# Part of a short convolution as float32 matmuls by diagonal matrices, and a state product for two column blocks at a time, in a kernel of attention and two feed-forward layers

## The chip, the core and the metric

The kernel runs on one core of one Trainium2 chip. The core has a matrix engine (TensorE, PE in the profile, with its weight loads as PEld), three engines for elementwise work (VectorE as DVE, ScalarE as ACT, GpSimd as POOL) and queues that start transfers (here all on SyncE, SP). Each engine works through its own instructions in a fixed order and waits on semaphores for the others. The metric is the time of one execution on the device in microseconds (us); lower is better.

## What is computed

Three stages follow each other. B = 8 batches, H = 8 heads, S = 512 tokens, Ns = 32 state tokens, D = 64; the feed-forward layers have a model width of 512 and an inner width of 1024. The weights and the taps of the convolution come as float64, the rest as float32.

```python
# 1: attention both ways between tokens x and a state
a     = softmax(scale * x @ state.T);   xread = a @ state
a2    = softmax(scale * state @ x.T);   sread = a2 @ x
y     = concat(xread, sread)            # 576 tokens, heads side by side: 512 wide
# 2: feed-forward with a convolution over three tokens as its gate
h     = relu(y @ w_in)                  # 1024 wide
conv  = cw[0] * h[t-1] + cw[1] * h[t] + cw[2] * h[t+1]      # per column, zeros at the ends
z     = (h * sigmoid(conv)) @ w_out
# 3: feed-forward with a mix of each token and the one before it
out   = sigmoid(xr @ w_r) * (relu(xk @ w_k) ** 2 @ w_v)
```

## The kernel before

**Precision.** Nearly every large product runs in float32r, a reduced form of float32, with each operand split into a high and a low part. `mm3` issues three matmuls for one product: high by high (L112), high by low (L113), low by high (L114). The float64 weights are split on the chip by `Weights.split`: two ACT instructions (L158 absolute value, L164 sign) and six DVE instructions (L160, L161, L165, L166, L169, L170) on 128x1024 for each piece of two blocks. There are four pieces of w_in and four of w_out; two staging buffers are shared by them, so a piece is loaded when the piece two before it has been split.

**Layout.** In stage 2 the columns of h are cut into KF = 8 blocks of 128 (f), and a block stands with its 128 columns on the partitions and 512 tokens along the row. Tiles t = 0 to 7 are the 512 token rows of a batch each; tile 8 holds the state rows of all batches. A slot (t, f) goes through five steps: `g1_main` (the product hps on PE), `g1_a` (Relu to hb on ACT, then the convolution), `g1_b` (sigmoid on ACT, times h on POOL for tile 0 and on DVE otherwise, tile g), `g1_c` (g split into gs, high on ACT, low on POOL for tiles 0 to 2) and `g1_sec` (twelve matmuls into four accumulators acc). The convolution is one ACT instruction for the first tap (L441) and two SCALAR_TENSOR_TENSOR on DVE for the others (L443), each over 128x512.

**The state product.** xread @ w_in isn't formed from xread. The state is first multiplied into w_in (`Attention.m`, tile p_m in PSUM, then me or m_odd in SBUF, as high and low), and hps is the attention matrix aring by that product. For batch 0, `m(q, f0, 1)` makes one block of 128 columns at a time: twelve matmuls over 128 columns, an ACT eviction (L274) and a DVE subtraction (L275). From batch 2 on, pairs of batches share the work (`pair_m`, L234), and the results are moved to me and m_odd by DMA (L237).

**PSUM.** hps has two buffers (tag h), p_m and the small products of the attention share two (tag at), and four hold the accumulators.

**What sets the order.** The program emits slots in order and gives each group of instructions a priority (`tc.cur_priority`): 1000 per slot plus a number for the step, with the attention and the weights hung in at half slots (`at_half`). A scheduler then puts the instructions of each engine in one fixed order, by these priorities and its own times. On the start, the SP queue carries the first state, x, the first piece of w_in, the taps (`vec.load`, two transfers), mu and the first piece of w_out.

Of the kernel before, what the change touches and what calls it, by code (L numbers as in the profile page):

```python
# [8 lines left out]
F32 = mybir.dt.float32  # L9
# [3 lines left out]
AF = mybir.ActivationFunctionType  # L13
ALU = mybir.AluOpType
AX = mybir.AxisListType

LOW_ON_POOL = (0, 1, 2)
GATE_ON_POOL = (0,)


BASE = 100000
# [9 lines left out]
def tile_kernel(  # L31
# [26 lines left out]
    nc = tc.nc  # L58
    B, P, NST, H, D = x_n.shape
    KC, S = x_t.shape[1], x_t.shape[3]  # L60
    NS = st_bd.shape[2] // (2 * KC)
    KF = w_in.shape[0]
# [23 lines left out]
    op = ctx.enter_context(tc.tile_pool(name="op", bufs=1))  # L86
    dp = ctx.enter_context(tc.tile_pool(name="dp", bufs=1, space=bass.MemoryType.DRAM))
    ps_acc = ctx.enter_context(tc.tile_pool(name="ps_acc", bufs=1, space=bass.MemoryType.PSUM))
    ps_h = ctx.enter_context(tc.tile_pool(name="ps_h", bufs=2, space=bass.MemoryType.PSUM))
# [6 lines left out]
    ident = const.tile([P, P], F32, name="ident")  # L96
    vcol = const.tile([P, 3 * KF], F32, name="vcol")
# [95 lines left out]
    def load_s(b, ap):  # L193
        sT[b] = ap.tile([P, KC, 2, NS], F32, tag="sT", name="sT", bufs=3)
        nc.sync.dma_start(out=sT[b].rearrange("p c u n -> p (c u n)"), in_=st_bd[b])

    def load_t(b, ap):
        xT[b] = ap.tile([P, KC, S], F32, tag="xT", name="xT", bufs=1)
        for c in range(KC):
            nc.sync.dma_start(out=xT[b][:, c], in_=x_t[b, c])  # L200
# [203 lines left out]
    def width(t):  # L404
        return S if t < B else B * Z - 2
# [18 lines left out]
    def g1_a(t, f):  # L424
        n = width(t)
        s = st1[t, f]
        hb = s["hb"] = cp.tile([P, N + 2], F32, tag="hb", name="hb", bufs=3)
        if t < B:
            nc.gpsimd.memset(hb[:, 0:S + 2:S + 1], 0.0)  # L429
            nc.scalar.activation(hb[:, 1:1 + S], s["p"], AF.Relu)  # L430
            nc.gpsimd.tensor_copy(carry[:, f, t], hb[:, S - 1:S + 1])
        else:
            v = hb[:, :B * Z].rearrange("p (b n) -> p b n", b=B)
            nc.gpsimd.tensor_copy(v[:, :, 0:2], carry[:, f])
            nc.gpsimd.memset(v[:, :, NS + 2:], 0.0)
            nc.scalar.activation(
                v[:, :, 2:NS + 2], s["p"][:, :B * NS].rearrange("p (b n) -> p b n", b=B), AF.Relu
            )
        a = s["a"] = cp.tile([P, N], F32, tag="acc", name="cacc")
        w = [vcol[:, k * KF + f:k * KF + f + 1] for k in range(3)]  # L440
        nc.scalar.activation(a[:, :n], hb[:, 0:n], AF.Copy, scale=w[0])  # L441
        for k in (1, 2):
            nc.vector.scalar_tensor_tensor(  # L443
                a[:, :n], hb[:, k:k + n], w[k], a[:, :n], op0=ALU.mult, op1=ALU.add
            )

    def g1_b(t, f):
# [3 lines left out]
        nc.scalar.activation(g[:, :n], s["a"][:, :n], AF.Sigmoid)  # L451
        eng = nc.gpsimd if t in GATE_ON_POOL else nc.vector
        eng.tensor_tensor(g[:, :n], g[:, :n], s["hb"][:, 1:1 + n], op=ALU.mult)
# [146 lines left out]
    def at_half(k, *fns, prio=None):  # L600
        p = 500 * k - AHEAD if prio is None else prio
        half.setdefault(k, []).extend((fn, p) for fn in fns)
# [9 lines left out]
    vec = Weights([conv], 1, 3 * KF, const, "c")  # L612
    vs = const.tile([P, 2, 3 * KF], F32R, name="vs")
    load_s(0, ap)
    load_t(0, ap)
    win[0][0]()
    vec.load()
    nc.sync.dma_start(out=muc, in_=mu)
    wout[0][0]()
    make_identity(nc, ident)  # L620
# [1 line left out]
    a = Attention(0, ap)  # L622
    a.scores([ps_acc.tile([P, 512], F32, tag=f"acc{g}", name="p_s") for g in range(G)])
    a.begin()
    win[0][1]()
    a.state()
    a.m(0, 0, 1)
    for g in range(G):
        a.max1(g, nc.vector)
    for g in range(G):  # L630
# [7 lines left out]
        a.norm1(g, nc.vector)  # L638
    for g in range(G):
        a.turn1(g)  # L640
    vec.split(vs.rearrange("p l (o n) -> p l o n", o=1))
    nc.vector.tensor_tensor(vcol, vs[:, 0].bitcast(F32), vs[:, 1].bitcast(F32), op=ALU.add)
    nc.vector.tensor_scalar(om, muc, scalar1=-1.0, scalar2=1.0, op0=ALU.mult, op1=ALU.add)
    wout[0][1]()

# [35 lines left out]
    def weight_at(w, need, at):  # L681
        at_half(at, w[0], w[1], prio=500 * need - WEIGHT_AHEAD)
# [4 lines left out]
    for f in range(1, KF):  # L687
        if f % 2 == 0:
            weight_at(win[f // 2], 2 * f - 1, max(0, 2 * f - 5))
        at_half(2 * f - 1, lambda f=f: a.m(f // 2, f % 2, 1))  # L690
    for f in range(2, KF, 2):
        weight_at(wout[f // 2], 2 * f + 5, 2 * f + 2)
    at_half(0, lambda: load_s(1, ap), lambda: load_t(1, ap), prio=-500)
# [2 lines left out]
    for b in range(1, B):  # L696
# [3 lines left out]
        (2, t, f) for t in range(NT2) for f in range(KF)  # L700
    ]
    FN = {1: (g1_main, g1_a, g1_b, g1_c, g1_sec), 2: (g2_main, g2_a, g2_b, g2_c, g2_sec)}
    p2 = None
    for i in range(len(slots) + 2):
        if i < len(slots):
            ph, t, f = slots[i]
            if (ph, t, f) == (1, B - 1, 2):
                ap_cm.__exit__(None, None, None)
                p2 = ctx.enter_context(tc.tile_pool(name="p2", bufs=1))
                for k in range(0, KF, 2):  # L710
                    w = weight(w_k, "k", "wk", p2, k, 2, 2)
                    h = h2 + 2 * k
                    weight_at(w, h, h - 4)
                for k in range(0, KF, 2):
                    w = weight(w_v, "v", "wa", wp, k, 2, 4)
                    h = h2 + 2 * k + 4
                    weight_at(w, h + 1, h - 3)
                for k in range(0, KC, 2):
                    w = weight(w_r, "r", "wb", wp, k, 2, 2)
                    h = h2 + 8  # L720
# [84 lines left out]
```

## Time and profile before

| | us |
|---|---|
| median of 3 runs (898.67 to 899.33) | 899.1 |
| the profiled execution | 901.15 |
| its span from first to last instruction | 899.2 |
| PE busy in the span | 850.8 (95%) |
| DVE busy | 564.0 (63%) |
| ACT busy | 531.2 (59%) |
| POOL busy | 118.8 (13%) |
| mean granted clock of PE | 0.974 of full |

The shares are averages over stages that differ: PE's 95% says little on the first 75 us, and DVE's 63% holds a stretch in which it is full. So such a profile is read by stretch first, then by the waits of the engine that ends last, then by the instructions around one place. "Idle before" is the time an engine stood still ahead of an instruction, with what ended it. Durations of one engine overlap by some hundredths of a microsecond, since its instructions are pipelined; what one costs in a full stretch is nearer to the distance between starts. PE clock 1.00 is 2.4 GHz and 0.50 is 1.2 GHz.

### The profile page before, as it was taken

The page shows a single profiled execution, that of the slowest core. Times are in us where ns is not written, and L with a number is a line of the kernel's source. Part 1 is how long each engine was busy: PE and PEld are TensorE (multiplying, and loading weights), DVE is VectorE, ACT ScalarE, POOL GpSimd, SP SyncE. Part 2 cuts the span into 40 slices and gives each one's busy share as a digit, 9 for nine tenths or more (in the row PEclk, how much of TensorE's full clock was granted, in tenths as well). Part 3 has the DMA queues.
Part 4 walks back from the last instruction along what each step waited for, and adds up shares of the span by engine and source line. Part 5 has one row for each costly group of instructions (what it writes and reads, how often), then busy time and mean ns, then how long its engine had stood idle before and what let it go on. Part 6 is the DMA issues. An engine that isn't in the chain of part 4 may idle for free.

```text
span 899.2 us, 12003 instructions
## 1 busy us (share of the span) xinstructions
PE 850.8 (95%) x4440; PEld 692.3 (77%) x4440; DVE 564.0 (63%) x950; ACT 531.2 (59%) x929; POOL 118.8 (13%) x223
## 2 busy tenths in 40 slices
PE   3749999999999997999999999999999999999997
PEld 1628777768777875789988888888888888888886
DVE  6899897699879987999784543523424244332221
ACT  4557686578577757777666755635556364553431
POOL 2313753342011112121000000000000000000000
PEclk7778999999999999999999999999999999999999
DMA  9682224544451537536731101111001111011010
GB/s 341 228 348 96 77 95 118 162 131 118 139 166 59 168 127 246 175 122 252 273 128 47 28 20 47 47 47 48 18 29 48 47 47 47 1 36 48 0 47 36
DMA packets 50842, 95.76 MB, mean 106 GB/s; under 512 B 9056, under 2 KB 31072, under 8 KB 48736
## 3 DMA queue, kind: packets, MB, share of 16 engines
q1 hardware_dynamic: 50784, 95.00, 32.0%
q8 instruction: 35, 0.57, 0.3%
q14 instruction: 23, 0.19, 0.1%
HBM read 64.54 MB, written 17.86 MB: 92 GB/s over the span
## 4 chain that ended last, share of the span: by engine, by line
PE 83%; DVE 8%; ACT 3%; issue 2%; DMA 2%; POOL 1%; SPq 0%; DVEq 0%; ACTq 0%; POOLq 0%
PE acc L113 13%; PE acc L114 13%; PE acc L112 13%; PE kps L112 7%; PE kps L113 7%; PE kps L114 7%; PE rps L114 3%; PE rps L113 3%; PE rps L112 3%; PE hps L112 3%; PE hps L114 3%; PE hps L113 3%; DVE cacc L443 2%; PE p_s L284 2%; PE p_m L113 1%
## 5 line engine op out<-in xcount | busy, mean ns | idle before, releaser
L568 DVE TENSOR_TENSOR ks<-k,ks 128x512 fp32r<-128x512 f32 (+1 forms) x72 | 47.7, 662 | 118.2 <-ACT ks L567 117.8
L443 DVE SCALAR_TENSOR_TENSOR cacc<-hb,vcol,cacc 128x512 f32<-128x512 f32 (+1 forms) x144 | 111.8, 788 | 15.5 <-ACT cacc L441 14.9
L113 PE MATMUL acc<-gs,out 128*128 128x512 f32 (+1 forms) x288 | 110.6, 386 | 0.0
L112 PE MATMUL kps<-xk,k 128*128 128x512 f32 (+1 forms) x288 | 110.0, 384 | 0.2 <-ACT k L554 0.2
L113 PE MATMUL kps<-xk,k 128*128 128x512 f32 (+1 forms) x288 | 110.2, 382 | 0.0
L114 PE MATMUL kps<-xk,k 128*128 128x512 f32 (+1 forms) x288 | 109.8, 382 | 0.0
L114 PE MATMUL acc<-gs,out 128*128 128x512 f32 (+1 forms) x288 | 109.6, 384 | 0.0
L112 PE MATMUL acc<-v,ks 128*128 128x512 f32 x272 | 106.0, 392 | 0.0
L113 PE MATMUL acc<-v,ks 128*128 128x512 f32 x272 | 105.9, 389 | 0.0
L114 PE MATMUL acc<-v,ks 128*128 128x512 f32 x272 | 105.7, 392 | 0.0
L112 PE MATMUL acc<-gs,out 128*128 128x512 f32 (+1 forms) x288 | 94.3, 389 | 4.3 <-ACT gs L459 4.3
L533 DVE SCALAR_TENSOR_TENSOR mix<-yt,muc,mix 128x384 f32<-128x384 f32 (+7 forms) x128 | 61.1, 500 | 47.7 <-ACT mix L531 47.2
L567 ACT ACTIVATE ks<-k 128x512 fp32r<-128x512 f32 (+1 forms) x72 | 43.6, 605 | 69.8 <-PE acc L114 69.6
L531 ACT ACTIVATE mix<-yt,om 128x384 f32<-128x384 f32 (+7 forms) x128 | 61.5, 517 | 32.2 <-DMA yt<-y 15.8
L554 ACT ACTIVATE k<-kps 128x512 f32<-128x512 f32 (+1 forms) x72 | 40.9, 569 | 48.9 <-PE kps L114 48.7
L112 PEld LDWEIGHTS acc<-gs,out 128*128 128x128 f32 x288 | 53.7, 192 | 16.1 <-ACT gs L459 6.1
L113 PEld LDWEIGHTS acc<-gs,out 128*128 128x128 f32 x288 | 54.8, 190 | 12.8 <-POOL hb L429 0.8
L114 PEld LDWEIGHTS acc<-gs,out 128*128 128x128 f32 x288 | 54.9, 191 | 10.8 <-issue 0.8
L112 PEld LDWEIGHTS kps<-xk,k 128*128 128x128 f32 x288 | 54.1, 188 | 10.8 <-ACT k L554 0.7
L113 PEld LDWEIGHTS kps<-xk,k 128*128 128x128 f32 x288 | 54.4, 189 | 10.1
L114 PEld LDWEIGHTS kps<-xk,k 128*128 128x128 f32 x288 | 54.3, 188 | 10.1
L451 ACT ACTIVATE g<-cacc 128x512 f32<-128x512 f32 (+1 forms) x72 | 43.8, 609 | 27.5 <-DVE cacc L443 19.4
(133 smaller groups left out, 1771.3 us busy)
## 6 DMA issues: line engine op xcount, KB each, us to landing
out<-r SPq DMA_DIRECT2D x34, 256.0 KB, 2.1
xT<-x_t SPq DMA_DIRECT2D x32, 256.0 KB, 4.0
xn<-x_n SPq DMA_DIRECT2D x8, 1024.0 KB, 5.4
y<-yo SPq DMA_DIRECT2D x8, 1024.0 KB, 4.8
me<-m SPq DMA_DIRECT2D x48, 128.0 KB, 2.4
m_odd<-m SPq DMA_DIRECT2D x48, 128.0 KB, 2.4
raw<-w_in SPq DMA_DIRECT2D x8, 512.0 KB, 6.0
raw<-w_out SPq DMA_DIRECT2D x8, 512.0 KB, 5.7
```

The source lines that it names most:

```text
L112: nc.tensor.matmul(ps, lh, rh, start=start and k == 0, stop=False)
L113: nc.tensor.matmul(ps, lh, rl, start=False, stop=False)
L114: nc.tensor.matmul(ps, ll, rh, start=False, stop=stop and k == last)
L284: nc.tensor.matmul(self.v["s", g][NS * j:NS * (j + 1), :], sT[self.b][r, h // 2, h % 2], xT[self.b][r, h // 2], start=True, stop=True,)
L443: nc.vector.scalar_tensor_tensor(a[:, :n], hb[:, k:k + n], w[k], a[:, :n], op0=ALU.mult, op1=ALU.add)
L451: nc.scalar.activation(g[:, :n], s["a"][:, :n], AF.Sigmoid)
L531: nc.scalar.activation(tmp[:, o:o + m], y[:, c, q - 1:q - 1 + m], AF.Copy, scale=om[:, i:i + 1])
L533: nc.vector.scalar_tensor_tensor(tmp[:, o:o + m], y[:, c, q:q + m], muc[:, i:i + 1], tmp[:, o:o + m], op0=ALU.mult, op1=ALU.add,)
L554: nc.scalar.activation(k[:, :n], s["p"][:, :n], AF.Relu)
L567: nc.scalar.activation(ks[:, 0, :n], s["k2"][:, :n], AF.Copy)
L568: nc.vector.tensor_tensor(ks[:, 1, :n], s["k2"][:, :n], ks[:, 0, :n].bitcast(F32), op=ALU.subtract)
```

## The change

For the first five blocks of tile 0 the convolution goes to PE. Each tap of a block becomes a 128x128 diagonal matrix (tile diag, fifteen of them, made by ACT from the identity matrix), and three float32 matmuls, not float32r, add the three shifted copies of hb into a PSUM tile cps of tag h; the sigmoid reads cps. Blocks 5 to 7 of tile 0 and all other tiles keep L441 and L443. For that the taps are loaded ahead of x and split ahead of all other DVE work. And `m` of batch 0 makes two blocks per call: half as many matmuls, each over 256 columns, and half as many evictions, each over 128x512.

```diff
+CONV_ON_PE = 5
...
+        if t == 0 and f < CONV_ON_PE:
+            a = s["a"] = ps_h.tile([P, 512], F32, tag="h", name="cps")
+            for k in range(3):
+                nc.tensor.matmul(a, diag[:, 3 * f + k], hb[:, k:k + S], start=k == 0, stop=k == 2)
+            return
         a = s["a"] = cp.tile([P, N], F32, tag="acc", name="cacc")
...
     load_s(0, ap)
+    vec.load()
     load_t(0, ap)
     win[0][0]()
-    vec.load()
...
+    vec.split(vs.rearrange("p l (o n) -> p l o n", o=1))
+    nc.vector.tensor_tensor(vcol, vs[:, 0].bitcast(F32), vs[:, 1].bitcast(F32), op=ALU.add)
+    diag = op.tile([P, 16, P], F32, tag="o8", name="diag")
+
+    def diagonals(f):
+        for k in range(3):
+            nc.scalar.activation(diag[:, 3 * f + k], ident, AF.Copy, scale=vcol[:, k * KF + f:k * KF + f + 1])
+
     win[0][1]()
     a.state()
-    a.m(0, 0, 1)
+    a.m(0, 0, 2)
...
-    vec.split(vs.rearrange("p l (o n) -> p l o n", o=1))
-    nc.vector.tensor_tensor(vcol, vs[:, 0].bitcast(F32), vs[:, 1].bitcast(F32), op=ALU.add)
+    diagonals(0)
...
         if f % 2 == 0:
             weight_at(win[f // 2], 2 * f - 1, max(0, 2 * f - 5))
-        at_half(2 * f - 1, lambda f=f: a.m(f // 2, f % 2, 1))
+            at_half(2 * f - 1, lambda f=f: a.m(f // 2, 0, 2))
+        if f < CONV_ON_PE:
+            at_half(2 * f - 1, lambda f=f: diagonals(f))
```

The lines of the changed kernel stand 2 lines lower up to the convolution and 7 to 16 lower behind it, so that L443 before has no counterpart for these blocks, L160 is L162, L164 is L166 and L451 is L458.

DVE around the first two blocks' convolution and the second piece of w_in, before (in_153 and out_222 are the split weights, cacc the convolution):

```order
L170 SCALAR_TENSOR_TENSOR out_222<-mid,raw 128x1024
L443 SCALAR_TENSOR_TENSOR cacc<-hb,vcol,cacc 128x512 x2
L160 TENSOR_SCALAR raw<-raw 128x1024
L169 TENSOR_SCALAR mid<-mid 128x1024
L161 TENSOR_SCALAR raw<-raw 128x1024
L165 TENSOR_TENSOR in_153<-raw 128x1024
L443 SCALAR_TENSOR_TENSOR cacc<-hb,vcol,cacc 128x512
L166 TENSOR_SCALAR raw<-in_153 128x1024
L443 SCALAR_TENSOR_TENSOR cacc<-hb,vcol,cacc 128x512
L371 TENSOR_SCALAR sr<-p_sr,s_151 128x128
L170 SCALAR_TENSOR_TENSOR in_153<-mid,raw 128x1024
```

The same place now:

```order
L172 SCALAR_TENSOR_TENSOR out_226<-mid,raw 128x1024
L162 TENSOR_SCALAR raw<-raw 128x1024
L171 TENSOR_SCALAR mid<-mid 128x1024
L163 TENSOR_SCALAR raw<-raw 128x1024
L167 TENSOR_TENSOR in_163<-raw 128x1024
L168 TENSOR_SCALAR raw<-in_163 128x1024
L172 SCALAR_TENSOR_TENSOR in_163<-mid,raw 128x1024
```

The four convolution instructions are gone, and sr (L371) has moved behind this piece.

ACT at the same place, before (g is the gate, L158 and L164 are the weight split's two steps):

```order
L430 ACTIVATE hb<-hps 128x512
L441 ACTIVATE cacc<-hb,vcol 128x512
L158 ACTIVATE raw<-raw 128x1024
L356 ACTIVATE a2T<-p_a_311 128x512
L430 ACTIVATE hb<-hps 128x512
L164 ACTIVATE raw<-raw 128x1024
L451 ACT_TABLE_LOAD
L451 ACTIVATE g<-cacc 128x512
```

And now:

```order
L358 ACTIVATE a2T<-p_a_303 128x512
L432 ACTIVATE hb<-hps 128x512
L160 ACTIVATE raw<-raw 128x1024
L458 ACT_TABLE_LOAD
L458 ACTIVATE g<-cps 128x512
L166 ACTIVATE raw<-raw 128x1024
L432 ACTIVATE hb<-hps 128x512
```

The sigmoid of the first block (L451, now L458) and its table load have moved ahead of the weight split's second step, and the second block's Relu behind both.

PE where the third block's second product begins, before (acc are the accumulators, with out_496 the split piece of w_out):

```order
L112 MATMUL hps<-aring,me_108 128x512
L113 MATMUL hps<-aring,me_108 128x512
L112 MATMUL acc_435<-gs,out_496 128x512
L112 MATMUL acc_436<-gs,out_496 128x512
L112 MATMUL acc_437<-gs,out_496 128x512
L112 MATMUL acc_438<-gs,out_496 128x512
L112 MATMUL p_m<-in_339,aux 128x128
```

And now:

```order
L116 MATMUL p_m<-in_334,aux 128x256
L444 MATMUL cps<-hb,diag 128x512 x3
L114 MATMUL acc_430<-gs,out_479 128x512
L114 MATMUL acc_431<-gs,out_479 128x512
L114 MATMUL acc_432<-gs,out_479 128x512
L114 MATMUL acc_433<-gs,out_479 128x512
L114 MATMUL p_m<-in_163,aux 128x256
```

The fourth block's convolution (cps) now stands directly ahead of the third block's second product, and that block's hps, of which two matmuls stood here, is all ahead of it.

## Rows read from the trace of the kernel before

**Rows 1.** Busy us (instructions): PE, PEld, DVE, ACT, POOL; PE clock, DMA share, GB/s.

```profile
30.00:50.00 20.00, 13.57 (x120) 9.78 (x123) 16.84 (x19) 12.42 (x16) 6.98 (x9) 0.91 0.64 241
50.00:75.00 25.00, 14.00 (x61) 10.76 (x54) 24.76 (x42) 15.29 (x21) 6.92 (x6) 0.59 0.74 283
75.00:130.00 55.00, 54.59 (x351) 44.46 (x350) 50.58 (x74) 39.44 (x69) 31.99 (x42) 1.00 0.25 86
130.00:200.00 70.00, 64.88 (x432) 49.08 (x431) 53.31 (x90) 45.24 (x76) 26.72 (x43) 1.00 0.47 132
```

**Rows 2.** Waits of PE up to 200 us: total us, times, longest.

```profile
PE p_srT L380 <- ACT e L315: 8.4, 1, 8.4
...
PE hps L112 <- DMA me<-m: 3.1, 2, 1.5
```

**Rows 3.** Timeline (start, us, engine, line, operation): exponentials, third block.

```profile
60.60 0.68 ACT L315 ACTIVATE e<-p_s,s 128x512 f32<-128x512 f32 x1
...
67.39 0.63 ACT L459 ACTIVATE gs<-g 128x512 fp32r<-128x512 f32 x1 [1.70 <-POOL g L453]
...
68.08 2.07 PE L112 MATMUL acc<-gs,out 128*128 128x512 f32 x4 [1.11 <-ACT gs L459]
```

**Rows 4.** Busy time by stretch, columns as in rows 1: the half clock.

```profile
60.00:74.50 14.50, 11.14 (x42) 9.46 (x43) 14.39 (x27) 9.65 (x15) 5.23 (x4) 0.50 0.62 227
```

**Rows 5.** Timeline of PE at 134 us.

```profile
134.24 0.44 PE L354 MATMUL p_a<-ident,e 128*128 128x128 f32 x2 [0.43 <-DVE m L234]
```

**Rows 6.** By shape, 28-90 us (xcount, busy us, mean ns); then timelines.

```profile
L443 DVE SCALAR_TENSOR_TENSOR cacc<-hb,vcol,cacc 128x512 f32<-128x512 f32 x11 | 12.3, 1116 | 2.6 <-ACT cacc L441 2.5
...
56.66 0.75 DVE L443 SCALAR_TENSOR_TENSOR cacc<-hb,vcol,cacc 128x512 f32<-128x512 f32 x1
...
86.28 1.78 DVE L443 SCALAR_TENSOR_TENSOR cacc<-hb,vcol,cacc 128x512 f32<-128x512 f32 x1
...
85.78 1.74 POOL L461 TENSOR_TENSOR gs<-g,gs 128x512 fp32r<-128x512 f32 x1 [1.27 <-ACT gs L459]
```

**Rows 7.** Timeline of ACT, DVE and SP around the second piece of w_in.

```profile
30.06 0.60 ACT L430 ACTIVATE hb<-hps 128x512 f32<-128x512 f32 x1 [1.17 <-PE hps L114]
...
33.29 1.18 ACT L164 ACTIVATE raw<-raw 128x1024 f32<-128x1024 f32 x1
...
35.41 1.22 DVE L165 TENSOR_TENSOR in<-raw 128x1024 fp32r<-128x1024 f32 x1 [0.53 <-DVE raw L161]
...
41.92 0.33 SPq L138 DMA_DIRECT2D raw<-w_out  x1
...
48.96 1.14 ACT L158 ACTIVATE raw<-raw 128x1024 f32<-128x1024 f32 x1 [4.29 <-DMA raw<-w_out]
```

**Rows 8.** By shape, 28-90 us: low part of the state product, DVE.

```profile
L275 DVE TENSOR_TENSOR me<-p_m,me 128x256 fp32r<-128x256 f32 x6 | 2.5, 416 | 0.0
```

**Rows 9.** Timeline of ACT and SP at the start.

```profile
4.34 0.51 ACT L255 ACTIVATE aux<-sT 128x128 fp32r<-128x128 f32 x2
11.60 0.63 ACT L321 ACTIVATE q<-q 128x512 f32<-128x512 f32 x1 [6.76 <-DVE q L309]
...
5.23 0.54 SPq L138 DMA_DIRECT2D raw<-conv  x1
```

**Rows 10.** Timeline of PE: products of 128 and 256 columns, and scores.

```profile
78.33 0.28 PE L114 MATMUL p_m<-in,aux 128*128 128x128 f32 x1
78.44 0.28 PE L112 MATMUL p_m<-in,aux 128*128 128x128 f32 x1
...
83.07 0.28 PE L113 MATMUL p_m<-in,aux 128*128 128x256 f32 x1
83.19 0.29 PE L114 MATMUL p_m<-in,aux 128*128 128x256 f32 x1
...
107.23 1.94 PE L284 MATMUL p_s<-xT,sT 64*32 64x512 f32 x16
109.11 0.50 PE L112 MATMUL hps<-aring,m_odd 128*128 128x512 f32 x1
```

## The prediction, made before the change was run

> **What bounds the kernel now.** I read the busy time by stretch first [rows 1]. The reader should see two regimes. From 75 us on TensorE (PE) has no idle time to speak of, at full clock: 54.6 of 55 us busy up to 130 us, 64.9 of 70 us up to 200. Before that VectorE (DVE) is full and PE is not: between 50 and 75 us DVE works 24.8 of 25 us and PE 14.0, at a mean granted clock of 0.59. So the kernel is a feed phase, in which DVE splits float64 weights, runs the attention of two batches and the convolution, and then a long matmul stream. Whatever ends the feed phase earlier by x us moves the whole stream by x, and whatever adds work to PE after it is added to the end.
>
> The waits of PE name the feeder [rows 2]: the longest after the start, 8.4 us, is a transpose that waits until the exponentials have released a PSUM buffer, and these stand behind DVE's maxima. Then I followed the third block (number 2) of tile 0. Its gate lands as gs at 67.39 us, 1.70 us of ACT's idle time before it being POOL's product, and PE starts its second product at 68.08 us [rows 3]. From there PE never runs dry, but it runs at half clock: 0.50 over 60 to 74.5 us [rows 4]. 68.08 us is the place against which I set the change. A second place is 134 us, where PE has caught up with DVE again: a transpose waits 0.43 us for the state product's low part (L234) that DVE had in its queue [rows 5]. What DVE does not gain by then, PE cannot keep.
>
> **The change on DVE.** Ten SCALAR_TENSOR_TENSOR of L443 go. Eleven of them between 28 and 90 us took 12.3 us, 1.116 us each; an undisturbed one took 0.75 us, and one beside a POOL subtraction that ran from 85.78 to 87.5 us took 1.78 us [rows 6]. That extra time belongs to the collision with POOL, whose instructions all stay. The Trainium skill (GPSIMD Engine Reference, Specifications) says the same, that POOL shares its SBUF interfaces with VectorE and collides with instructions that have two SBUF inputs; by that rule the next DVE instruction pays, and the six below are worth 4.5 us and no more, which would make the time 893.3.
>
> - Blocks 2 to 4, six instructions: 6 x 0.75 = 4.5 us at least, 6 x 1.116 = 6.7 us at most. DVE has no idle time there [rows 1], so they count in full. I take 5.0, near the undisturbed price.
> - Blocks 0 and 1, four instructions: 3.0 us by the undisturbed price, but here DVE is busy 16.8 of 20 us, so part of it only turns into waiting. The wait that can take its place is visible in the order of ACT: the Sign step L164 of the second w_in piece, which started at 33.29 us and let DVE's product L165 start at 35.41 [rows 7], now stands behind the first sigmoid, which waits for the first convolution on PE. Relu ends at 30.7 us in either kernel; three float32 matmuls (2.8 us at full clock, 5.6 at half, below) end at 33.6 or 36.4, a sigmoid of 0.6 follows, and L164 starts at 34.3 to 37.1 instead of 33.29. L165 is then 0.1 to 2.9 us later than now (L164 takes 1.18), while the two convolution steps that stood between it and the end of that split (some 2.85 us with their collisions) are gone. The split ends 2.8 us earlier to 0.1 later. This is worth following, because the next w_out load is issued when it ends, at 41.92 us, and ACT waits 4.29 us for it, until 48.96 [rows 7]: a gain there is passed on by the load. I take 2.0, bounds -0.5 to 3.0.
> - The state product: eight evictions of 128x256 at 0.416 us [rows 8], 3.3 us, become four of 128x512. At the 0.75 us of the other 128x512 instruction that is 3.0, so 0.3 is saved; 0 to 1.7, between nothing and half.
> - The start: the two loads of the taps go ahead of the four of x. The first took 0.54 us of SP's time where it stood [rows 9], so two take some 1.1, and scores, maxima and the first weights all come behind them. I take -1.0, bounds -1.1 to 0. The taps' small DVE steps move with them into the time before the first transpose, in which DVE has nothing to do, so they cost nothing.
>
> Sum on DVE: 5.0 + 2.0 + 0.3 - 1.0 = **6.3 us**; ends 2.9 (4.5 - 0.5 + 0 - 1.1) and 11.4 (6.7 + 3.0 + 1.7).
>
> **On ACT.** Five L441 go, fifteen diagonals come. Two copies of 128x128 took 0.51 us, so fifteen take 15 x 0.255 = 3.8 us. The order puts all fifteen ahead of the first exponential, where ACT idles 6.76 us [rows 9]: taps landed by some 4.5 us (an estimate: the state, issued just ahead of them, let ACT copy it at 4.34), seven short DVE steps, diagonals from about 6.7 to 10.5, the exponential due at 11.6 plus the later start. Hidden, with 2 us to spare; without that cover up to 3.8 us on the first chain.
>
> **On PE.** The trace has no full float32 matmul. The nearest row is the score product: eight matmuls over 512 columns (two records each) held PE from 107.23 to 109.11 us [rows 10], 1.88 us. Run one after another that is 0.235 each, 0.7 a block; run four beside each other it is two rounds of 0.94. I take 0.94: each uses 64 rows and 32 columns of the array, and four of them don't overlap. The Trainium skill (FP8 and Floating Point Precision, TensorE Precision Notes) says that true FP32 makes four passes; float32r starts every 0.12 us at 256 columns, so by that rule one costs 4 x 0.24 = 0.96, and the low end is out. So a block costs 2.8 us at full clock and 5.6 at half, and five cost 14.1. On the other side 96 products of 128 columns become 48 of 256: they start every 0.11 us at 128 and every 0.12 at 256 [rows 10], so 5 us is saved at full clock. PE's work grows by 14.1 - 5 = 9 us. It pays only if it lies in PE's idle time: 11 us of idle between 50 and 75 and 6.4 between 30 and 50 [rows 1].
>
> For the place 68.08: in the new order the third block's convolution stands right behind the scores of batch 1, and what stands ahead of `acc` is exponentials, transposes, the product m (12 x 0.12 = 1.4 us, double at half clock) and the fourth block's convolution (2.8 or 5.6). Exponentials ended at 61.3 [rows 3]; 2 us earlier by DVE's gain is 59.3, plus 0.5 + 1.4 + 2.8 is 64.0, or 68 at half clock. So `acc` starts 0 to 4 us earlier; I take 3. What remains for PE after it differs by 48 narrow products (5.3 us) that become 12 wide ones (1.4), four `hps` already done (4 x 0.24 = 1.0), one convolution to come (2.8): 2 less. And the 6.4 us at half clock behind 68.08 cost 3.2 us; a PE that has worked through 50 to 64 us should have its clock up, so I take 3. PE's side: 3 + 2 + 3 = **8 us**, ends 2 and 9.4.
>
> PE can use no more than DVE feeds it by 134 us, so DVE's 6.3 stands. The profiled execution took 901.15 us, 1.95 of it outside its span of 899.2; the median of the runs is 899.1, 2.05 below. The difference carries over: 901.15 - 6.3 = 894.85 in a profiled run, 899.1 - 6.3 = **892.8 us**. Its own range is 889.7 (PE's end, 9.4) to 896.2 (DVE's end, 2.9).
>
> **Rivals.**
> 1. *PE stays at half clock.* The added matmuls don't raise the clock before 65 us, and the fourth block's take 5.6. Against: they fill the 8.4 us hole in which the clock fell. By the ends above PE gains 0 to 1 at `acc`, 2 behind it, and little of the clock: 2.5, so 896.6.
> 2. *The gain is swallowed later.* PE idles 5.1 us between 130 and 200 us [rows 1], 3.1 of it on copies of the state product by DMA [rows 2]. If PE only comes to these earlier and waits longer, all but 0.5 to 1 us goes: 898.4. For it: DVE is busy 50.6 of 55 us up to 130 and its gain early is uncertain. Against: the copies are issued behind evictions that move forward with PE and DVE; nothing in that chain has a time of its own.
> 3. *Slower: the matmuls are late and in the way.* PE takes its queue in order. If Relu of the fourth block comes only after the exponentials, and its convolution at half clock (5.6 us) stands ahead of `acc`, while DVE's side brings nothing early (its load-bound end), `acc` starts at 68.08 + 5.6 = 73.7 instead of 68.08; 2.0 less work and at most 1.2 of clock behind it give back 3.2: 899.1 + 2.4 = 901.5. It decides at 70.1 us: from an `acc` later than that the change loses. The two PSUM buffers that products and convolutions now share work the same way.
> That the change does not do what it says is excluded by the order: the ten instructions are gone from DVE.
>
> **How the numbers follow.** Forecast 0.68, rival 1 0.09, rival 2 0.12, rival 3 0.11. A measurement of this kernel can tell about 0.2% (1.8 us) from no change. Faster is forecast and rival 1: 0.77. Same is rival 2: 0.12. Slower 0.11. The range 888.5 to 899.5 takes in the first three with 1 us for what the reordered stream does beyond 140 us; it leaves out rival 3 and some 0.06 of better or worse tails.
>
> **What would show it.** Right: `acc` of block 2 on PE at 63 to 66 us, full clock from about 65 instead of 74.7, three convolution matmuls in 2.8 us, diagonals done before 12 us, the same 5 us of PE idle in the stretch that was 130 to 200. Wrong: a block's convolution of 5.6 us behind 50 us; L164 of the second piece after 37 us with the w_out load no earlier; PE's idle after 130 us grown by what was gained before.

## The result, and the profile after

The changed kernel took 892.42 us (median of 4, 891.25 to 893.08) against 898.88 for the kernel before beside it (898.47 to 899.33): a ratio of 0.9918, 95% interval 0.9895 to 0.994, so 6.5 us less. A second measurement (a2_again, below) gave 0.992 with 0.99 to 0.9939, so 7.2 us by the ratio and 5.9 by the medians. The forecast of 892.8 and its range held. The profiled execution took 893.08 us with a span of 891.1, 8.1 below that of before. What is taken from traces below comes from one execution of each kernel, which lies up to 2.3 us from that kernel's median. The traced execution of before lies 2.3 us above it and that of after 0.7, which is 1.6 of the 8.1. Ratios come from all executions.

The busy time by stretch, after, with the columns of rows 1:

```profile
30.00:50.00 20.00, 18.53 (x126) 10.96 (x126) 13.96 (x15) 10.29 (x13) 6.83 (x9) 0.89 0.65 250
50.00:75.00 25.00, 21.68 (x102) 14.93 (x99) 24.52 (x39) 16.74 (x25) 10.55 (x11) 0.93 0.75 280
75.00:130.00 55.00, 53.59 (x319) 40.99 (x319) 51.93 (x73) 37.96 (x66) 31.90 (x40) 1.00 0.25 84
130.00:200.00 70.00, 68.35 (x453) 52.22 (x452) 56.77 (x100) 50.00 (x85) 25.98 (x45) 1.00 0.48 132
```

Read against [rows 1], PE is busy 18.5 of 20 us where it had 13.6, and 21.7 of 25 where it had 14.0, at a granted clock of 0.93 instead of 0.59. DVE is as full between 50 and 75 us as it was. And between 130 and 200 us PE idles 1.65 us, not 5.1.

PE's waits up to 200 us, after (total us, times, longest), beside [rows 2]:

```profile
PE p_srT L382 <- ACT e L317: 3.1, 1, 3.1
...
PE cps L444 <- ACT hb L432: 1.5, 2, 0.8
```

The 8.4 us hole is 3.1, and the convolution's own waits are 1.5. PE's timeline around the third and fourth block, after:

```profile
52.88 2.74 PE L444 MATMUL cps<-hb,diag 128*128 128x512 f32 x6
...
56.62 0.40 PE L116 MATMUL hps<-aring,me 128*128 128x512 f32 x1
60.12 0.44 PE L382 MATMUL p_srT<-ident,sr 128*128 128x128 f32 x2 [3.09 <-ACT e L317]
...
62.87 3.81 PE L444 MATMUL cps<-hb,diag 128*128 128x512 f32 x6
66.11 1.50 PE L114 MATMUL acc<-gs,out 128*128 128x512 f32 x4
```

The transpose that waits for the exponentials starts 0.63 us earlier than before (60.12 against 60.75, which is the end of that wait), so the hole did not shrink because the exponentials came much earlier. It shrank from its front: the third block's convolution (52.88 to 55.05, the next start) lies in it, and behind that six matmuls of the next `hps`, the last of them the one at 56.62. The second product of that block, `acc`, starts at 66.11 us instead of 68.08 [rows 3]. The half clock, 60 to 74.5 us before [rows 4], is this short now:

```profile
62.00:64.50 2.50, 2.50 (x7) 1.53 (x7) 2.49 (x6) 2.48 (x5) 1.27 (x1) 0.50 0.99 387
64.50:75.00 10.50, 10.50 (x56) 8.44 (x55) 10.38 (x19) 6.51 (x10) 4.88 (x5) 0.98 0.59 224
```

The issue of the output transfer of tiles 0 and 3 on the SP queue (start, us) shows when the gain is made. After:

```profile
115.79 0.33 SPq L488 DMA_DIRECT2D y<-yo  x1
...
239.51 0.33 SPq L488 DMA_DIRECT2D y<-yo  x1
```

Before:

```profile
119.76 0.33 SPq L481 DMA_DIRECT2D y<-yo  x1
...
248.06 0.33 SPq L481 DMA_DIRECT2D y<-yo  x1
```

So 4.0 us are there at the end of tile 0, and 8.5 at the end of tile 3. Nothing was swallowed on the way; the lead grew.

**Where it went, as one account.** The span is PE's idle plus PE's busy time. Before: 48.4 + 850.8. After, by the first lines of the page:

```profile
span 891.1 us, 11958 instructions
...
PE 856.4 (96%) x4422; PEld 686.9 (77%) x4422; DVE 559.7 (63%) x936; ACT 529.9 (59%) x935; POOL 120.1 (13%) x223
```

That is 34.7 + 856.4. PE's idle time fell by 13.7 us and its busy time rose by 5.6. The convolution (L444) holds PE 16.7 us in that trace by its durations, so all its other work became 11.1 us shorter: by the wide state product (e1 below puts that at some 3) and, as the remainder, by the clock (some 8). The durations overlap what follows them; from start to next start the five blocks take 13.9 us, and then 8.3 us are left for the other work and some 5 for the clock. So the clock's part is an estimate by subtraction. This account, with durations, is used for the experiments (the traced executions of e2 and e3 lie 1.6 and 1.8 us above their kernels' medians, those of e4, e6 and e10 1.9, 2.2 and 1.5 below):

| kernel | span | PE idle | PE busy | of it convolution | all else |
|---|---|---|---|---|---|
| before | 899.2 | 48.4 | 850.8 | 0 | 850.8 |
| after | 891.1 | 34.7 | 856.4 | 16.7 | 839.7 |
| e1_conv_only | 894.4 | 34.7 | 859.7 | 15.8 | 843.9 |
| e2_m_only | 899.7 | 51.0 | 848.7 | 0 | 848.7 |
| e3_no_conv | 894.3 | 47.1 | 847.2 | 0 | 847.2 |
| e4_both | 892.7 | 38.8 | 853.9 | 15.6 | 838.3 |
| e6_blocks_2_4 | 892.9 | 44.1 | 848.8 | 8.5 | 840.3 |
| e10_twice | 903.1 | 36.7 | 866.4 | 30.1 | 836.3 |
| e8_all_blocks | 904.5 | 41.1 | 863.4 | 25.4 | 838.0 |

### The profile page after: what moved, and what is told of

Its sections match the earlier page's. It is cut to its first block, busy times and chain, and to the rows that moved or that the text cites. A ratio compares the mean times of both kernels' runs of the same rounds, so it can differ in the third digit from the quotient of the medians.

```text
span 891.1 us, 11958 instructions
## 1 busy us (share of the span) xinstructions
PE 856.4 (96%) x4422; PEld 686.9 (77%) x4422; DVE 559.7 (63%) x936; ACT 529.9 (59%) x935; POOL 120.1 (13%) x223
## 4 chain that ended last, share of the span: by engine, by line
PE 80%; DVE 12%; DMA 2%; issue 2%; ACT 2%; SPq 1%; POOL 1%; DVEq 0%; ACTq 0%
PE acc L115 12%; PE acc L114 12%; PE acc L116 12%; PE kps L114 7%; PE kps L115 7%; PE kps L116 7%; PE rps L116 3%; PE rps L115 3%; PE rps L114 3%; PE hps L114 3%; PE hps L116 3%; PE hps L115 2%; PE p_s L286 2%; DVE cacc L450 1%; DMA me<-m 1%
## 5 line engine op out<-in xcount | busy, mean ns | idle before, releaser
L450 DVE SCALAR_TENSOR_TENSOR cacc<-hb,vcol,cacc 128x512 f32<-128x512 f32 (+1 forms) x134 | 101.4, 767 | 6.5 <-ACT cacc L448 5.9
L115 PEld LDWEIGHTS acc<-gs,out 128*128 128x128 f32 x288 | 54.2, 188 | 15.0 <-issue 3.4
L114 PEld LDWEIGHTS acc<-gs,out 128*128 128x128 f32 x288 | 52.6, 188 | 16.7 <-ACT gs L466 4.6
L116 PEld LDWEIGHTS acc<-gs,out 128*128 128x128 f32 x288 | 54.2, 188 | 10.5 <-issue 0.8
L458 ACT ACTIVATE g<-cacc 128x512 f32<-128x512 f32 (+1 forms) x67 | 40.6, 606 | 33.0 <-DVE cacc L450 15.5
```

The costliest lines, as they stand in the source:

```text
L114: nc.tensor.matmul(ps, lh, rh, start=start and k == 0, stop=False)
L115: nc.tensor.matmul(ps, lh, rl, start=False, stop=False)
L116: nc.tensor.matmul(ps, ll, rh, start=False, stop=stop and k == last)
L450: nc.vector.scalar_tensor_tensor(a[:, :n], hb[:, k:k + n], w[k], a[:, :n], op0=ALU.mult, op1=ALU.add)
```

## The experiments

Theory A is the prediction's: a feeder, DVE, sets the time, and what it is spared comes out at the end. Theory B is PE's side: the convolution's matmuls fill the hole between 52 and 60 us, which keeps the clock up, and from 61 us PE is so full that each microsecond of its work counts. Each run was timed in five rounds beside the kernel before. Every variant also gets an order of its own from the scheduler, far behind tile 0 too; where a trace shows that such an order cost time, it is said.

**The two halves of the change.** e1_conv_only is the changed kernel with the narrow state product:

```diff
-    a.m(0, 0, 2)
+    a.m(0, 0, 1)
...
-            at_half(2 * f - 1, lambda f=f: a.m(f // 2, 0, 2))
+        at_half(2 * f - 1, lambda f=f: a.m(f // 2, f % 2, 1))
```

> The changed kernel, but the state product of batch 0 again for one column block at a time. Theory A (the feeder: the gain is DVE's relief, and the wide state product is worth 0.3 us): 892.8 us. Theory B (PE: the gain is less work and a full clock on PE; 48 narrow products behind the point where PE stops running dry cost 5.3 us, 12 wide ones 1.4): some 3.9 us of the gain goes, 896.3 us.

Measured: 0.9954 (0.9941 to 0.9966), 4.2 us faster than before; with 895.5 us it is nearer to B's number. e2_m_only is the reverse edit on the kernel before, with the wide product alone.

> The kernel before with the wide state product alone; convolution and loads as before. Theory A: 898.6 us (0.3 us less). Theory B: 3.9 us of PE's work behind 68 us goes, 895.0 us.

Measured: 1.0 (0.9988 to 1.0013): A's 0.3 lies inside the interval, B's 4 does not. So the wide product is worth nothing by itself, and some 3 us beside the convolution (0.9954 against 0.9918 and 0.992; 2 by the medians). The page's first lines of e1:

```profile
span 894.4 us, 12067 instructions
...
PE 859.7 (96%) x4470; PEld 694.6 (78%) x4470; DVE 554.8 (62%) x940; ACT 532.3 (60%) x939; POOL 117.5 (13%) x223
```

and of e2:

```profile
span 899.7 us, 11915 instructions
...
PE 848.7 (94%) x4392; PEld 685.6 (76%) x4392; DVE 565.8 (63%) x946; ACT 529.1 (59%) x925; POOL 122.1 (14%) x223
```

e1 has the same 34.7 us of idle PE as the changed kernel and 3.3 us more of busy PE: with PE full, what the wide product saves on PE is time. In e2 PE's busy time fell by 2.1 from before, and its idle time rose by 2.6: with PE waiting for its feeder, the same saving became idle time. An operation on the engine that is not yet the bound is worth nothing until another part of the change makes it the bound.

**Relief without the matmuls, and the matmuls without relief.** e3_no_conv leaves the convolution of the five blocks out:

```diff
-            a = s["a"] = ps_h.tile([P, 512], F32, tag="h", name="cps")
-            for k in range(3):
-                nc.tensor.matmul(a, diag[:, 3 * f + k], hb[:, k:k + S], start=k == 0, stop=k == 2)
+            s["a"] = hb[:, 1:1 + S]
             return
```

> The changed kernel without any convolution in the five blocks: the sigmoid reads h itself, so that neither DVE nor PE nor ACT does it (that part of the computation is left out). It shows DVE's relief without PE's cost and without PE's added activity. Theory A (PE's cost is hidden): within 1 us of the changed kernel, 891.5 to 892.5 us. Theory B: the last block's 2.2 us go, but PE has its idle stretch around 55 us back and runs at half clock behind it, 893 to 895 us.

Measured: 0.9944 (0.993 to 0.9958), 5.0 us faster than before; 894.5 us lies in B's range and not within 1 us of the changed kernel, as A had it. e4_both keeps the convolution on ACT and DVE and runs PE's matmuls besides, into a tile that nothing reads:

```diff
-            a = s["a"] = ps_h.tile([P, 512], F32, tag="h", name="cps")
+            extra = ps_h.tile([P, 512], F32, tag="h", name="cps")
             for k in range(3):
-                nc.tensor.matmul(a, diag[:, 3 * f + k], hb[:, k:k + S], start=k == 0, stop=k == 2)
-            return
+                nc.tensor.matmul(extra, diag[:, 3 * f + k], hb[:, k:k + S], start=k == 0, stop=k == 2)
```

> The changed kernel with the five blocks' convolution on PE as well as on ACT and DVE; the sigmoid reads the latter, PE's result is thrown away. PE's activity and clock without DVE's relief. Theory A: nothing of the relief is left, the start costs 1.0 us and the wide product gives 0.3: 899.6 us, or more where the matmuls are in the way. Theory B: clock and wide product remain, only the last block's matmuls cost: 893 to 895 us.

Measured: 0.9969 (0.9957 to 0.9981), 2.8 us faster than before, although PE has fifteen matmuls more and no other engine is spared the convolution; 896.6 us lies between the two theories. The two halves add up to 7.8, near the 6.5 and 7.2 of the whole change, though each holds the start, the diagonals and the wide product once. So both theories hold a part: the relief (of DVE, and of ACT's first tap) is worth about 5 with these three, and a kernel with work added to PE and no relief is 2.8 faster and not slower. Busy time by stretch between 50 and 75 us, for PE alone, of e2 and of e3, which have none of the convolution's matmuls:

```profile
50.00:75.00 25.00, 17.96 (x67) 0.73 0.64 235
...
50.00:75.00 25.00, 17.59 (x69) 0.73 0.82 315
```

and of e4:

```profile
50.00:75.00 25.00, 18.42 (x77) 0.93 0.67 250
```

The columns here are PE's busy time, its clock, DMA share and GB/s. With the matmuls the clock is 0.93 in that stretch, without them 0.73. In the account, the matmuls of e4 take 15.6 us more than e2 has, but the rest of PE's work is 10.4 shorter and idle time 12.2 less. That trace is the fastest of e4's six executions, 1.9 us below their median, so its size is generous; its direction is that of the ratio. That the matmuls alone did it is not shown: e4 differs from e2 in the start, the diagonals and the scheduler's order too, and no run separates these.

**The changed kernel again**, for the runs on that chip:

> The changed kernel once more, beside the parts on the same chip. Both theories: 6 to 7.5 us less than the kernel before.

Measured: 0.992 (0.99 to 0.9939).

**Which blocks.** e5_blocks_0_1 and e6_blocks_2_4 are the changed kernel with the convolution on PE for two or three blocks:

```diff
-        if t == 0 and f < CONV_ON_PE:
+        if t == 0 and 0 <= f < 2:
```

(and 2 <= f < 5 for e6).

> The changed kernel with only blocks 0 and 1 convolved on PE. Theory A (the prediction's terms): 2.0 for these blocks, 0.3 for the product, -1.0 for the start: 1.3 us less than before. Theory B (in the changed kernel's trace DVE begins the second w_out split at 50.34 us against 50.13, so these blocks relieve nothing; PE's hole at 52 to 60 us and the half clock behind it come back): 0 to 0.5 us less than before, or up to 1 more.

> The changed kernel with only blocks 2 to 4 convolved on PE. Theory A: 5.0 + 0.3 - 1.0 = 4.3 us less than before, 2 us more than the changed kernel. Theory B: these are the blocks whose matmuls fill the hole at 52 to 60 us and whose steps DVE is full with, so nearly the whole gain stays: 6.5 to 7.4 us less than before.

Measured: e5 1.0026 (1.001 to 1.0041), 2.3 us slower than before, which neither theory had; e6 0.9952 (0.9933 to 0.997), 4.3 faster (2.7 by the medians), which is A's number and not B's 6.5. The sum of both is 2.0, and the whole is 7.2: the runs don't add, but both hold the start and the wide product. Beside blocks 2 to 4, blocks 0 and 1 are worth 2.9. That they are worth nothing alone does not follow from e5, whose trace loses its time far behind them. The output transfers of tiles 5 and 6 on the SP queue, e5:

```profile
323.56 0.53 SPq L488 DMA_DIRECT2D y<-yo  x1
...
376.35 0.33 SPq L488 DMA_DIRECT2D y<-yo  x1
```

Before:

```profile
329.31 0.33 SPq L481 DMA_DIRECT2D y<-yo  x1
...
376.00 0.38 SPq L481 DMA_DIRECT2D y<-yo  x1
```

At tile 5 e5 is 5.75 us ahead of the kernel before, at tile 6 0.35 behind; the changed kernel is 8.0 ahead at both. What e5's two blocks bring is gone in that one stretch, in which e8 and e10 lose time too (below). The start was measured by itself. e7_taps_first is the kernel before with the taps loaded and split first, nothing else:

```diff
     load_s(0, ap)
+    vec.load()
     load_t(0, ap)
     win[0][0]()
-    vec.load()
...
     a.begin()
+    vec.split(vs.rearrange("p l (o n) -> p l o n", o=1))
+    nc.vector.tensor_tensor(vcol, vs[:, 0].bitcast(F32), vs[:, 1].bitcast(F32), op=ALU.add)
     win[0][1]()
```

> The kernel before with the taps loaded and split first, as the changed kernel has it, and no convolution on TensorE, no diagonals, no wide product. It measures the start alone. Theory A: the prediction's 1.0 us of a later start goes through to the end: 900.7 where before has 899.7. Theory B: the start is delayed by the 0.5 to 0.8 us seen in the changed kernel's first exponentials, but TensorE has idle time enough until 61 us to swallow it: 899.5 to 900. If it is 2 us or more slower, the start explains why blocks 0 and 1 alone were slower than before.

Measured: 1.0021 (1.001 to 1.0033), 1.9 us slower (1.5 by the medians). A's 1.0 lies at the interval's end, 0.9 to 3.0, and B's nothing is out. But its trace shows no later start. The first exponential (11.60 before, [rows 9]) and the Relu of the first block (30.06 before, [rows 7]) of e7:

```profile
11.67 0.63 ACT L321 ACTIVATE q<-q 128x512 f32<-128x512 f32 x1 [7.84 <-DVE q L309]
...
30.02 0.60 ACT L430 ACTIVATE hb<-hps 128x512 f32<-128x512 f32 x1 [1.17 <-PE hps L114]
```

So the 1.9 us are lost behind the start, and where they are lost stays open. They can't simply be added back to e5, e6 or e11.

**More on PE.** e8_all_blocks puts all eight blocks on PE (the diagonals of blocks 5 to 7 take the places of the first three):

```diff
-CONV_ON_PE = 5
+CONV_ON_PE = 8
...
-                nc.tensor.matmul(a, diag[:, 3 * f + k], hb[:, k:k + S], start=k == 0, stop=k == 2)
+                nc.tensor.matmul(a, diag[:, 3 * (f % 5) + k], hb[:, k:k + S], start=k == 0, stop=k == 2)
...
-            nc.scalar.activation(diag[:, 3 * f + k], ident, AF.Copy, scale=vcol[:, k * KF + f:k * KF + f + 1])
+            nc.scalar.activation(diag[:, 3 * (f % 5) + k], ident, AF.Copy, scale=vcol[:, k * KF + f:k * KF + f + 1])
```

> The changed kernel with all eight blocks of tile 0 convolved on PE, the diagonals of blocks 5 to 7 in the places of those of 0 to 2. Three more blocks cost PE 3 x 2.2 = 6.6 us where it no longer idles, and save DVE six steps of 0.75. Theory A (DVE feeds PE up to 134 us): the relief of 4.5 counts and the matmuls are partly hidden, 0 to 2 us less than the changed kernel. Theory B (PE never dry from 61 us): 4 to 6.6 us more than the changed kernel.

Measured: 1.0067 (1.0048 to 1.0087), 6.0 us slower than before and 13 slower than the changed kernel. A falls here: DVE has six instructions less, and the time goes up. It is B's direction, and beyond its size; 4.8 us of it have another cause, below. e9_four_blocks goes the other way (CONV_ON_PE = 4):

> The changed kernel with four blocks (0 to 3) on TensorE; block 4's three steps go back to ScalarE and VectorE. Theory A (the time follows what VectorE is spared): VectorE gets back the two steps of one block and its waits, a third of the 5.0 that the prediction gave to blocks 2 to 4, so 1.7 slower than the changed kernel: about 895.5 where that has 893.8. Theory B (TensorE is full from 61 us on, so each of its microseconds after that counts): block 4's matmuls, 2.2 us, are gone from a full engine, and the time is 1 to 2 us shorter than the changed kernel's: 891.5 to 893; the idle time of TensorE stays near 35 us and its busy time falls from 856 to about 854.

Measured: 0.9941 (0.9927 to 0.9955), 5.3 us faster than before. That is 1.9 less gain than with five blocks (0.6 to 1.2 by the medians), near A's 1.7; the intervals overlap a little. B's shorter time did not come: without block 4's matmuls PE's idle time is 40.1 us instead of 34.7 to 35.7, so what PE was spared became waiting. e10_twice leaves DVE as in the changed kernel and doubles PE's part:

```diff
-            for k in range(3):
-                nc.tensor.matmul(a, diag[:, 3 * f + k], hb[:, k:k + S], start=k == 0, stop=k == 2)
+            for k in range(6):
+                nc.tensor.matmul(a, diag[:, 3 * f + k % 3], hb[:, k % 3:k % 3 + S], start=k == 0, stop=k == 5)
...
+    hid = const.tile([P, P], F32, name="hid")
+    nc.scalar.activation(hid, ident, AF.Copy, scale=0.5)
...
-            nc.scalar.activation(diag[:, 3 * f + k], ident, AF.Copy, scale=vcol[:, k * KF + f:k * KF + f + 1])
+            nc.scalar.activation(diag[:, 3 * f + k], hid, AF.Copy, scale=vcol[:, k * KF + f:k * KF + f + 1])
```

> The changed kernel with each convolution on TensorE done twice with halved diagonals into the same sum: 15 float32 matmuls more, at the 0.74 us that one took at full clock 11 us of TensorE's work, nothing else. Theory A (a feeder sets the time; the convolution's matmuls stand largely beside it): only what delays the state product of block 2 counts, two blocks' 4.4 us, less the 1.7 that the prediction saw TensorE's sum above VectorE's: 2.5 to 4.5 slower than the changed kernel, 896.5 to 898. Theory B (TensorE is full): all but the idle time that it had in 30 to 61 us, some 3 us, counts: 7 to 9 slower, 901 to 903, idle time down to about 32 us and busy time up by 10 to 11.

Measured: 1.0073 (1.0057 to 1.0089), 13.8 us slower than the changed kernel by the ratios (12.5 to 13.1 by the medians); both theories said less. The page's first lines:

```profile
span 903.1 us, 12018 instructions
...
PE 866.4 (96%) x4452; PEld 693.7 (77%) x4452; DVE 559.0 (62%) x936; ACT 534.3 (59%) x938; POOL 125.1 (14%) x223
```

PE's busy time is up by 10.0 from the changed kernel's, and its idle time, which B saw fall to 32, is 36.7. PE's idle time by stretch (us) shows that two things are mixed in this:

| kernel | 0 to 61 | 61 to 200 | 200 to 330 | 330 to 390 |
|---|---|---|---|---|
| before | 30.1 | 8.1 | 0.0 | 5.3 |
| after | 21.3 | 3.1 | 0.6 | 4.8 |
| e5_blocks_0_1 | 25.3 | 10.0 | 1.9 | 8.4 |
| e8_all_blocks | 21.7 | 1.7 | 3.3 | 9.6 |
| e10_twice | 19.0 | 2.7 | 0.8 | 9.4 |
| e11_taps_late | 21.0 | 9.6 | 0.2 | 6.4 |

Up to 330 us the second fifteen matmuls found 2.6 us of idle time, where the change had taken 13.2 from the kernel before. So of their 10.0 us some 7.4 count, which is B's 7 to 9. The other 4.6 us came late, between 330 and 390 us, where e8 has 4.8 more than the changed kernel. There PE waits in e8 for one small product of the attention, sr:

```profile
PE p_srT L382 <- DVE sr L373: 4.4, 1, 4.4
```

The changed kernel has 4.8 us of waits in that stretch, none for sr. What DVE does at that place, in e8:

```profile
348.37 0.70 DVE L171 TENSOR_SCALAR mid<-mid 128x1024 uint32<-128x1024 uint32 x1 [4.65 <-DMA mid<-w_k]
...
350.97 0.35 DVE L373 TENSOR_SCALAR sr<-p_sr,s 128x128 f32<-128x128 f32 x1
```

In e10:

```profile
345.44 0.69 DVE L171 TENSOR_SCALAR mid<-mid 128x1024 uint32<-128x1024 uint32 x1 [2.83 <-DMA mid<-w_k]
...
348.04 0.35 DVE L373 TENSOR_SCALAR sr<-p_sr,s 128x128 f32<-128x128 f32 x1
```

And in the changed kernel:

```profile
335.99 0.35 DVE L373 TENSOR_SCALAR sr<-p_sr,s 128x128 f32<-128x128 f32 x1
```

There sr stands ahead of that step of w_k's split, which follows at 346.38 us. In e8 and e10 the scheduler put the step first, DVE stood 4.65 and 2.83 us for its load, and sr, with PE behind it, came after, though in e8 PE had its input ready by 344.8 us. PE's wait for sr is 4.4 us in e8 and 2.6 in e10. It comes from DVE's order there, not from the work that was added to PE 200 us before. e5 loses in the same stretch (8.4 us idle), without a wait of PE for sr; what delays it there stays open.

**The diagonals' cover.** e11_taps_late is the changed kernel with the taps loaded and split where the kernel before has it:

```diff
     load_s(0, ap)
-    vec.load()
     load_t(0, ap)
     win[0][0]()
+    vec.load()
...
         a.turn1(g)
+    vec.split(vs.rearrange("p l (o n) -> p l o n", o=1))
+    nc.vector.tensor_tensor(vcol, vs[:, 0].bitcast(F32), vs[:, 1].bitcast(F32), op=ALU.add)
     diagonals(0)
```

> The changed kernel with the taps loaded and split where the kernel before does it (after the first piece of w_in and after the first softmax), so that the start is as before and the fifteen diagonals are made on ScalarE from about 21 us on, when it has other work, no longer in its wait at the start. Theory A: the start's 0.5 to 0.8 us come back, and the diagonals cost ScalarE 4.5 us beside the splits, of which VectorE feels about 1: 893 to 894.5, no change from the changed kernel. Theory B: the first block's matmuls come later by up to the 4.5 us, in a stretch where TensorE has idle time; from 61 us on nothing differs: 893 to 894, first acc of block 2 near 66 us. Both say that the diagonals' place is worth under 1 us; 2 us or more slower would mean that the idle time at the start is what pays for them.

Measured: 0.9956 (0.9943 to 0.9969), 3.2 us slower than the changed kernel by the ratios (1.5 to 2.1 by the medians); both theories had it under 1. The timeline of ACT of e11:

```profile
10.83 0.63 ACT L323 ACTIVATE q<-q 128x512 f32<-128x512 f32 x1 [6.14 <-DVE q L311]
...
26.38 4.50 ACT L636 ACTIVATE diag<-ident,vcol 128x128 f32<-128x128 f32 x15 [1.47 <-DVE vcol L655]
30.78 0.58 ACT L432 ACTIVATE hb<-hps 128x512 f32<-128x512 f32 x1
```

and of the changed kernel at its start:

```profile
5.26 4.49 ACT L638 ACTIVATE diag<-ident,vcol 128x128 f32<-128x128 f32 x15 [1.44 <-DVE vcol L633]
12.36 0.63 ACT L323 ACTIVATE q<-q 128x512 f32<-128x512 f32 x1 [2.61 <-DVE q L311]
```

e11 starts its exponentials 1.5 us earlier, and the 4.50 us now stand right ahead of the first block's Relu, which starts 0.75 us later than the changed kernel's (30.03 us). In the changed kernel the same work lies in a wait of which 2.61 us are left over. But this does not explain the loss. Up to 61 us PE idles no more in e11 than in the changed kernel (table above), and `acc` of block 2 starts 6.5 us earlier (59.58 us), since PE's order there is another one. PE's busy time, clock, DMA share and GB/s behind that, e11 and the changed kernel:

```profile
61.00:200.00 139.00, 129.44 (x820) 1.00 0.37 115
...
61.00:200.00 139.00, 135.94 (x837) 0.99 0.41 125
```

PE idles 6.5 us more there, long after the diagonals. What their place alone is worth stays open.

## Why the prediction was right, and where its steps were not

**The place that decides.** `acc` of block 2 at 63 to 66 us was forecast, 66.11 was found: 2.0 earlier instead of 3. Full clock from about 65 us was forecast, and it is there from 64.5. What rivals 1 and 3 needed, a PE at half clock and an `acc` later than 70.1, did not come. But the place does not decide the time. The same instruction in e11, e8 and e5:

```profile
59.58 1.49 PE L114 MATMUL acc<-gs,out 128*128 128x512 f32 x4
...
63.38 1.49 PE L114 MATMUL acc<-gs,out 128*128 128x512 f32 x4
...
65.22 1.08 PE L114 MATMUL acc<-gs,out 128*128 128x512 f32 x4
```

All three are earlier than 66.11; e11 gained less than the changed kernel, and e8 and e5 were slower than the kernel before.

**Blocks 2 to 4 (5.0).** The price near the undisturbed instruction was the right choice: e6 gives 4.3 and e3 5.0, each with the start in it, and e6 with PE's part too. Why not the 6.7 of the mean of [rows 6] can be read from two pairs. Before, DVE and POOL:

```profile
38.72 1.78 DVE L443 SCALAR_TENSOR_TENSOR cacc<-hb,vcol,cacc 128x512 f32<-128x512 f32 x1
...
38.39 1.56 POOL L461 TENSOR_TENSOR gs<-g,gs 128x512 fp32r<-128x512 f32 x1 [0.58 <-ACT gs L459]
```

After:

```profile
38.29 1.80 DVE L168 TENSOR_SCALAR raw<-in 128x1024 uint32<-128x1024 uint32 x1
...
38.26 1.27 POOL L468 TENSOR_TENSOR gs<-g,gs 128x512 fp32r<-128x512 f32 x1
```

POOL's subtraction stands at the same time, and where it stretched a convolution step from 0.75 us it now stretches a step of the weight split, which took 0.68 at 47.06 us with no POOL instruction beside it. The same over 28 to 90 us, by shape (xcount, busy us, mean ns), before:

```profile
L161 DVE TENSOR_SCALAR raw<-raw 128x1024 uint32<-128x1024 uint32 x6 | 5.2, 861 | 0.0
...
L166 DVE TENSOR_SCALAR raw<-in 128x1024 uint32<-128x1024 uint32 x3 | 2.1, 689 | 0.0
```

And the same two steps after:

```profile
L163 DVE TENSOR_SCALAR raw<-raw 128x1024 uint32<-128x1024 uint32 x6 | 6.2, 1040 | 0.0
...
L168 DVE TENSOR_SCALAR raw<-in 128x1024 uint32<-128x1024 uint32 x3 | 3.2, 1057 | 0.1
```

These nine instructions alone took 2.1 us more than before. The Trainium skill (GPSIMD Engine Reference, Specifications) says that POOL shares its SBUF interfaces with VectorE; that the next DVE instruction would pay, as the prediction drew from it, is what the trace shows, and the 893.3 that followed from it is as near to the measured medians as the 892.8 that was forecast.

**Blocks 0 and 1 (2.0).** The step failed at its place. The Sign step of the second w_in piece started at 35.83 us, inside the forecast 34.3 to 37.1, and DVE waited for it:

```profile
37.00 1.26 DVE L167 TENSOR_TENSOR in<-raw 128x1024 fp32r<-128x1024 f32 x1 [3.42 <-ACT raw L166]
```

The next w_out load was issued at 41.37 instead of 41.92 [rows 7], and DVE began its split at 50.34 us, where the kernel before had 50.13. Nothing was passed on by the load. What makes these blocks worth 2.9 beside the others is not shown. PE's work in its idle time up to 61 us (30.1 us before, 21.3 after) would be PE's sum and not DVE's, but the scheduler's other order is a rival, and e5 is spoilt by its late loss.

**The wide product (0.3).** e2 gives 0.0 alone, and e1 gives 3 beside the convolution. The prediction had both numbers, 0.3 on DVE and 5 us of PE's work saved, and took DVE's; with PE full it is PE's that counts.

**The start (-1.0).** The delay was there and was gone by the first block. The first exponential started 0.76 us later in the changed kernel (12.36 against 11.60 [rows 9]), but the Relu of the first block, which started at 30.06 before [rows 7], is as early as it was (the wide product, which makes that block's input, may have its part in this):

```profile
30.03 0.60 ACT L432 ACTIVATE hb<-hps 128x512 f32<-128x512 f32 x1 [3.83 <-PE hps L116]
```

e7's 1.9 us have another cause, which stays open.

**The diagonals (nothing).** Right: 4.49 us against a forecast 3.8, done at 9.75 us, before 12. Whether they would cost "up to 3.8" without that cover, e11 can't tell.

**A float32 matmul (0.94 at full clock).** Mis-sized: the blocks whose matmuls ran at full clock took 2.28 and 2.17 us from their first start to the next instruction's, 0.72 to 0.76 a matmul, so a block costs 2.2 and not 2.8. The four passes of the Trainium skill (FP8 and Floating Point Precision, TensorE Precision Notes) gave 0.96 by the same rows; the measured price is about three of the 0.24 that a float32r matmul of 512 columns took. What the half clock added (4.06 us for the first block, 3.24 for the fourth) made up for it: 13.9 us from start to next start for all five where 14.1 was forecast, which is luck.

**"PE can use no more than DVE feeds it by 134 us."** This is the step that failed in the sum: the stretch behind 130 us was to have the same 5 us of idle PE, and it has 1.65; the lead grew from 4.0 us at the end of tile 0 to 8.5 at the end of tile 3. PE's sum of 8 meets the trace's 8.1 by luck, since 1.6 of that are the two traced executions; DVE's 6.3 is near the timed 6.5 and 7.2, but of its four terms 2.0 and -1.0 did not happen where they were placed. The forecast was near because the two sums differed by 1.7 only and because these terms cancelled in part. Its picture of one binding engine was too simple: e3 and e10 show that DVE's relief counts and that most of PE's work counts in the same kernel. With four blocks the one still gives; with eight PE's 7.0 us of added work and the late loss have taken back more than all of it.

A version better than the changed kernel was not found: four and eight blocks, late taps and the narrow product are all slower in the median.

## What to carry to other kernels

Before work is moved to an engine with idle time, add up how much of it lies in that idle time and how much behind the point from which the engine is full: here fifteen matmuls paid, and fifteen more found idle time for 2.6 of their 10.0 us. Price a step that is taken off an engine at its undisturbed duration: here, what stretched it stretched its neighbour. Look in the trace for where a variant loses its time before its time is put down to its edit, since the scheduler's order changes with it; three of the kernels here (e5, e8, e10) lost 3 to 5 us more than 200 us behind the edited place. And time a change's parts together as well as alone, because a saving on an engine that waits shows only once another part has filled that engine.

## What was not expected of the hardware

A true float32 matmul of 128x128 by 512 columns took 0.72 to 0.76 us at full clock, about three float32r matmuls of that size and not four. A kernel with work without any use on PE (e4) was 2.8 us faster than the kernel before, with the granted clock of 50 to 75 us at 0.93 instead of the 0.73 of e2. A one-input step of 128x1024 on DVE that takes 0.68 us took 1.80 beside a POOL subtraction.
